# FNet and H3 in one kernel: where the items of the inverse stage stand beside the hidden-DFT pieces, and how many rounded inputs are kept ready

## The chip, the core and the metric

The kernel runs on one NeuronCore of one Trainium2 chip. The metric is the device time of one execution in microseconds (us), as the median of several runs. The core has five engines that run side by side, each with its own queue of instructions in program order: PE (TensorE, matmuls; its weight loads are shown apart as PEld), DVE (VectorE), ACT (ScalarE), POOL (GpSimd) and SP (SyncE). In this kernel SP does nothing but issue transfers, POOL issues a few transfers besides small arithmetic, and ACT issues some of the stores.

## The reference, cut to what matters

```python
x = A_x                                   # 1 x 2048 x 576, float32
x = x + A(_layernorm(x))                  # first layer
x = x + B(_layernorm(x), k, v, shift_k, ssm_k, ssm_D)
x = x + A(_layernorm(x))                  # second layer
x = x + B(_layernorm(x), k, v, shift_k, ssm_k, ssm_D)

def A(x):                                 # FNet: real part of a 2-D DFT
    a = x @ dft_hid_re.T; b = x @ dft_hid_im.T
    return dft_seq_re @ a - dft_seq_im @ b

def B(q, k, v, shift_k, ssm_k, ssm_D):    # H3
    kv = short_causal_conv(k, shift_k) * v
    y = irfft(rfft(kv, 4096) * rfft(ssm_k, 4096))[:2048] + kv * ssm_D
    return q * y
```

The factor y of B does not depend on q, so it is computed once and used in both layers.

## The kernel before, in words

The sequence is cut into 16 blocks of 128 rows. Matrix products are made in fp32r from two parts of each factor: a rounded high part, which ACT writes, and the low part that is left, which DVE gets by a subtraction. The helper `split` (L97) makes both; in the stage of interest it is `act_split` (L518), whose ACT half is issued through `act` (L511), so that all ACT instructions of the stage keep the order in which they are written.

The first layer's sequence DFT is the loop `layer` (L302): 128 steps numbered n, each with 12 matmuls 128x512 into four accumulators named s and two into one named rm. Every second step of a stretch, a **W piece** is put in (`finish`, L293; `hidden`, L278): 27 matmuls 128x288 of the hidden DFT, in a row, into one PSUM bank of the tag bk, which DVE then adds to the residual (L289). The tag bk has three banks, and the items below use them too.

Between the steps the kernel works off the long convolution as a list of 96 items, `feeds` (L570 and on), written by the generator `branch`. The middle items (64) transform, multiply and transform back; the inverse items (32, called kind 1 or inverse items here) finish the transform. Ten inverse items are spread among the last middle items, and 22 come after the last middle item, which has number 73; these are the items 74 to 95. An inverse item (`i2_products`, L552) is:

- four matmuls 128x288 into two bk banks, from a coefficient tile (`fc`, loaded by POOL, L586 through L173) and from the rounded input, high and low part (`df`);
- for each bank one ACT copy of half the partitions (L560, through L514), one DVE addition of the other half (L561) and one store by SP (L562).

After its products item i has the input of item i+2 rounded (`split_feed(i + 2)`, L618) and the raw input of item i+6 loaded by SP (`load_feed`, L577). There are three `df` tiles of 1152 words, four landing tiles, four `fc` tiles in this last part and four output tiles `vo`. The raw inputs of the items from 80 on are columns of `v_d[1]`, to which the last middle item writes too, so the load for item 80 needs the store of the last inverse product of the middle stage (L550, issued by ACT).

When an item is written into the program is set by two counters in the main loop (L788 to L818): `passed` grows by a share of 3.2 for each step and by 3.6 for each W piece, `spent` by the item's own cost (2.0 for an inverse item), and items are written as long as `spent` lags behind. At a W piece the piece is written first, 3.6 is added, and the items that have come due follow. The items' instructions are tied behind the DVE addition of the latest W piece and the latest evacuation of the accumulators (`behind(*added, *evac)`). A list scheduler then gives each engine its final order: it takes instructions in the order in which they are written, but lets one that is ready go ahead of one that its own timing model believes not yet ready.

Walking through the counters gives the order in which the last items and W pieces are written. Before the change:

| step n | written, in order, at the end of the step |
|---|---|
| 101 | item 74 inside the step; W, 75, 76 |
| 103 | item 78 inside; W, 79, 80 |
| 105 | item 83 inside; W, 84, 85 |
| 107 | item 88 inside; W, 89, 90 |
| 109 | item 92 inside; W, 93, 94 |

The other items stand inside the steps between. The last W piece of the block comes after step 110 and all items.

At the last middle item (L630) the tiles of the middle stage that are no longer needed are given to the inverse stage. One SBUF region of 6144 words holds, in this order: three `df` tiles (0 to 3456), the middle stage's matrices `mc` (3456 to 3968), two tiles `yf` of its rounded products (3968 to 4544 and 4544 to 5120), two `fc` tiles (5120 to 5632). Before the change two more `fc` tiles of 256 words are laid from 3968 on, over the first `yf`.

Of the kernel before, what the change touches and what calls it, by code (L numbers as in the profile page):

```python
# [15 lines left out]
P = 128  # L16
HP = P // 2
S = 2048
D = 576
# [26 lines left out]
I2_LATE = 6  # L46
I2_COST = 2.0
PIECE = 3.6
STEP = 3.2
KP = 4  # L50
H = 2 * P
# [15 lines left out]
def fnet_h3_kernel(ctx: ExitStack, tc: tile.TileContext, x, c_mat, w_re, w_im, k_pad, v, shift_k,  # L67
# [34 lines left out]
    @contextmanager  # L102
    def behind(*instructions):
        with ExitStack() as stack:
            for i in instructions:
                stack.enter_context(tc.issue_after(i))
            yield
# [185 lines left out]
    def finish(pending, pieces):  # L293
        while pending and pieces:
            if not isinstance(pending[0], types.GeneratorType):
                pending[0] = hidden(*pending[0])
            if next(pending[0], 0) == 0:
                pending.pop(0)
            else:
                pieces -= 1  # L300

    def layer(get_x, xres, done, pending, blocks=TB):  # L302
        steps = [(g, tb, k) for tb in range(blocks) for g in range(2) for k in range(J)]
        for n, (g, tb, k) in enumerate(steps):
            for i in range(2):
                if n == 0 and steps[i] not in CT:
                    load_c(steps[i])
            if n + 2 < len(steps):
                load_c(steps[n + 2])
            for i in range(XLEAD + 1 if blocks == TB else 1):  # L310
                if n + i < J:
                    get_x(n + i)
            if k == 0:
                ps = list(acc4)
                ps.append(psp.tile([P, NT], F32, tag="rm", name="rm"))
            c = CT.pop(steps[n])
            first, last = k == 0, k == J - 1
            while last and g == 0 and pending:
                yield n, None
            for dc in range(NC):  # L320
                xh = X[k][:, dc * P:(dc + 1) * P]
                xl = X[k][:, D + REM + dc * P:D + REM + (dc + 1) * P]
                mm(ps[dc], xh, c[0], first, False)
                mm(ps[dc], xh, c[1], False, False)
                seq[:] = [mm(ps[dc], xl, c[0], False, last)]
                if dc == NC // 2 - 1:
                    yield n, False
                elif blocks == TB and dc < NC - 1 and n >= MID_FROM and not last:
                    yield n, "part"
                if last:  # L330
                    (evac_u if blocks == TB else save_u)(g, ps, dc)
            xr = X[k][:, NC * P:D + REM]
            mm(ps[NC], xr, c[0], first, False)
            seq[:] = [mm(ps[NC], xr, c[1], False, last)]
            if last and blocks < TB:
                store_r(tb, g, ps[NC])
            elif last:
                evac_r(g, ps)
                if g == 1:
                    us = dict(U)  # L340
                    pending.extend([us, tb, jj, xres, done] for jj in range(TB))
            yield n, True
# [8 lines left out]
    def branch():  # L351
# [224 lines left out]
        def load_feed(i):  # L576
            if i < len(feeds):  # L577
                kind, hf, q = feeds[i]
                landed[i] = ring["land"]()
                load_after(two(landed[i]) if kind else landed[i], v_d[hf][:, q::J, :] if kind else  # L580
                           t_d[4 * q:4 * q + 4, :, hf * D:(hf + 1) * D].rearrange("m j d -> (m j) d"))

        def load_fc(k):
            if k < len(rows):
                fcs[k] = two(ring["fc"]())
                load_fr(fcs[k], i2c[rows[k]])  # L586

        def split_feed(i):
            if i < len(feeds):
                halves[i] = parts("df")  # L590
                act_split(*halves[i], landed.pop(i))
# [6 lines left out]
        for i in range(2):  # L598
            split_feed(i)
            load_feed(i + 3)  # L600
        used, ahead, feed_ahead, product = 0, 2, 3, None
        for i, (kind, hf, q) in enumerate(feeds):
            df = halves.pop(i)
            if kind:
                i2_products(hf, q, fcs.pop(used), df)
                load_fc(used + ahead)
                used += 1
            else:
                kk = mid_kernel(df)
                yield 1.6  # L610
                p1 = mid_signal(df, kk)
                if len(yfs) == MID_LAG:
                    yield 1.1
                    mid_inverse(*yfs.pop(0))
                if product is not None:
                    yfs.append((*product[:2], mid_round(product[2])))
                product = hf, q, p1
            split_feed(i + 2)  # L618
            if i >= I2_FIRST - 8 and feed_ahead == 3:
                tiles = [ring["land"]() for _ in range(3)]  # L620
                if tiles[0] is third:
                    ring["land"], feed_ahead = Ring(tiles[1:]), 2
                    lay(m1, fc_at, ("fc", 2 * P, 2))
                    load_fc(0)
                    load_fc(1)
            if feed_ahead == 2:
                feed_ahead = 2.5
            else:
                load_feed(i + int(feed_ahead) + 2)
            if i == last_mid:  # L630
                yfs.append((*product[:2], mid_round(product[2])))
                while yfs:
                    yield 0.4
                    mid_inverse(*yfs.pop(0))
                for name, t, at, words in (("fc", m1, spare, 2 * P), ("land", flts, kk_at, D)):
                    old = ring[name]
                    held = [old.tiles[(old.n + m) % 2] for m in range(2)]
                    fresh(name)
                    lay(t, at, (name, words, 2))
                    ring[name].tiles.extend(held)  # L640
                for m in range(2):
                    load_fc(used + ahead + m)
                    load_feed(i + ahead + 3 + m)
                ahead = feed_ahead = 4
            yield I2_COST if kind else 0.4

    def sums(src, junk):
# [140 lines left out]
    spent = passed = 0.0  # L788
    total = (I2_END + 1 - MID_FROM) * STEP + 3 * 2 * TB * PIECE
    work = 64 * 3.1 + 32 * I2_COST  # L790
    for n, whole in layer(get_x0, lambda j: x[:, j, :], done0, pending):
        part = whole == "part"
        if part:
            whole = False
        if (whole or whole is not None and n % J < J - 1) and n <= F1_END and not part:
            at = n if whole else n - 0.5
            at16 = 4 + 2 * F1_16
            want = int(4 + F1_16 * at / 8 if at <= 16 else at16 + (68 - at16) * (at - 16) / (F1_END - 16))
            with behind(made[min(n + 2, J - 1)], *evac):
                while used < want:  # L800
                    next(br)
                    used += 1
        if whole is not None and not part and n >= W_FROM and len(W) < 9:
            with behind(*stored):
                next(wl)
        if whole and n == MID_LOAD:
            with behind(*asked):
                next(br)
        if n >= MID_FROM:
            if whole is not None:  # L810
                share = (5 if whole else 3) if n % J < J - 1 else (8 if whole else 6)
                passed += STEP * share / 14 * BORDER.get(n % J, 1.085)
            if whole is None or whole and n % 2 == 1 and n % (2 * J) < J - 1 and pending:
                finish(pending, 1)
                passed += PIECE
            while spent < work * min(1.0, passed / total):
                with behind(*added, *evac):
                    spent += next(br, work)  # L818
        if not whole:
            continue  # L820
        if n >= W_SAVE and n % 2 == 0:
            next(wl, 0)
        m = n - PREP
        if m == 0:
            lay(flts, SC_AT + CRAW * NT + 2 * D, ("xa", D, 2), ("yb", D, 2))
            old = ring["craw"]
            held = [old(), old()]
            fresh("craw")
            lay(flts, SC_AT + CRAW * NT + 6 * D, ("craw", NT, 1))
            ring["craw"].tiles.extend(held)  # L830
            gate = region_b(F32, "gate")
            lay(gate, 0, ("xa", D, 4), ("yb", D, 4), ("xj", D, 2))
        if 0 <= m and n < HOLD:
            advance(m // 2 if m % 2 == 0 and m < 2 * EARLY else None)
# [340 lines left out]
```

## Time and profile before

| what | us |
|---|---|
| median of three runs (1180.59, 1182.12, 4165.63) | 1182.12 |
| the profiled execution, its own time | 1181.27 |
| its span, from the first instruction to the last | 1179.5 |
| PE busy | 1167.0 |
| DVE busy | 867.0 |
| ACT busy | 647.6 |
| POOL busy | 75.7 |

The profiled execution's own time is 1.8 us over its span. In the trace the stretch of the inverse items after item 74 goes from 538 to 597 us. Times in the views count from the start of the span. The ends of matmuls are modelled, so a matmul looks longer than the distance to the next one's start, and PE looks busy while it waits for a short time; its losses are read from the distances between starts.

### The profile page before, as it was taken

What the parts mean: (1) busy time and instruction counts of PE and PEld (TensorE: products, weight loads), DVE (VectorE), ACT (ScalarE), POOL (GpSimd) and SP (SyncE); (2) the same over time, 40 slices, a digit from 0 to 9 for tenths busy, and PEclk for the clock granted to TensorE, in tenths of its full rate; (3) what the DMA queues carried; (4) which work ended last, traced back from release to release, by engine and by line L of the source; (5) the groups of instructions that cost most, each with busy time, mean ns of one, the idle gap of its engine ahead of it and who ended that gap; (6) DMA issues with size and microseconds to landing.
All of it is one profiled execution on the core that took longest, in us unless ns stands there. A gap on an engine that the chain in (4) does not pass through costs nothing.

```text
span 1179.5 us, 18144 instructions
## 1 busy us (share of the span) xinstructions
PE 1167.0 (99%) x6198; PEld 988.8 (84%) x6198; DVE 867.0 (74%) x1564; ACT 647.6 (55%) x1280; POOL 75.7 (6%) x115
## 2 busy tenths in 40 slices
PE   8999999999999999999999999999999999999997
PEld 6776667988899888888888898888888888889997
DVE  7899983788777778877757766865776777774764
ACT  7865655577766667766645666534444445450210
POOL 2310000000000000001101111000000000001111
PEclk9999999999999999999999999999999999999999
DMA  9879898456656666648956777762762777795621
GB/s 325 297 228 308 263 292 291 156 153 177 215 196 211 198 181 193 192 140 241 286 185 215 249 250 239 241 236 89 252 240 72 233 273 259 263 323 164 201 103 41
DMA packets 147455, 255.67 MB, mean 217 GB/s; under 512 B 16161, under 2 KB 56353, under 8 KB 147362
## 3 DMA queue, kind: packets, MB, share of 16 engines
q1 hardware_dynamic: 111890, 210.17, 55.7%
q10 hardware_dynamic: 28560, 37.91, 9.1%
q0 software_dynamic: 6912, 6.43, 2.4%
q8 instruction: 49, 0.80, 0.3%
q14 instruction: 44, 0.36, 0.1%
HBM read 187.80 MB, written 66.65 MB: 216 GB/s over the span
## 4 chain that ended last, share of the span: by engine, by line
PE 90%; DVE 4%; DMA 3%; ACT 2%; issue 1%; SPq 0%; POOL 0%; DVEq 0%; ACTq 0%
PE s L76 52%; PE bk L76 29%; PE rm L76 6%; PE bf L76 2%; DMA flts<-in_ssm_k 1%; DMA t<-ud 1%; DVE f1f L395 1%; ACT flts L514 1%; DVE mid L520 0%; DVE mats L100 0%; DVE f1f L400 0%; DMA early<-in_x 0%; DVE u L100 0%; DMA vd<-flts 0%; DMA flts<-vd 0%
## 5 line engine op out<-in xcount | busy, mean ns | idle before, releaser
L76 PE MATMUL s<-mats 128*128 128x512 f32 x2102 | 549.4, 395 | 4.3 <-ACT mats L197 2.3
L76 PEld LDWEIGHTS s<-mats 128*128 128x128 f32 x2102 | 382.0, 188 | 84.6 <-issue 10.7
L100 DVE TENSOR_TENSOR mats<-flts,mats 128x512 fp32r<-128x512 f32 x206 | 140.9, 688 | 50.4 <-ACT mats L99 46.1
L99 ACT ACTIVATE mats<-flts 128x512 fp32r<-128x512 f32 x206 | 128.1, 627 | 78.9 <-PE bk L76 34.3
L514 ACT ACTIVATE flts<-bk 128x288 f32<-128x288 f32 (+1 forms) x192 | 78.5, 409 | 101.6 <-PE bk L76 83.4
L76 PE MATMUL bk<-mid 128*128 128x288 f32 x704 | 131.1, 301 | 0.3
L76 PEld LDWEIGHTS bk<-mid 128*128 128x128 f32 x704 | 110.7, 188 | 22.0 <-ACT flts L514 5.1
L76 PE MATMUL bk<-w,u 128*128 128x288 f32 x864 | 119.9, 295 | 0.1
L76 PEld LDWEIGHTS bk<-w,u 128*128 128x128 f32 x864 | 117.5, 188 | 2.7 <-ACT flts L514 0.8
L520 DVE TENSOR_TENSOR mid<-flts,mid 128x576 fp32r<-128x576 f32 (+1 forms) x149 | 92.2, 624 | 5.9 <-ACT mid L514 4.2
L76 PE MATMUL rm<-mats 128*128 128x512 f32 x304 | 94.6, 391 | 0.3 <-DVE flts L275 0.3
L514 ACT ACTIVATE mid<-flts 128x576 fp32r<-128x576 f32 (+1 forms) x148 | 79.5, 574 | 1.8 <-DVE flts L561 0.7
L289 DVE TENSOR_TENSOR flts<-flts,bk 128x288 f32<-128x288 f32 x48 | 21.8, 453 | 72.6 <-PE bk L76 72.6
L76 PE MATMUL bk<-mats 128*128 128x288 f32 (+1 forms) x376 | 67.8, 317 | 0.0
L76 PEld LDWEIGHTS rm<-mats 128*128 128x128 f32 x304 | 56.9, 188 | 12.9 <-PE s L76 0.7
L453 ACT ACTIVATE flts<-bf 128x384 f32<-128x384 f32 (+1 forms) x104 | 43.2, 462 | 43.9 <-PE bf L76 42.5
L76 PE MATMUL s<-t,mats 128*128 128x512 f32 x264 | 65.2, 390 | 0.1
L186 POOL TENSOR_TENSOR flts<-flts 128x1 f32<-128x1 f32 x34 | 28.0, 824 | 518.2 <-DVE flts L185 515.8
L76 PE MATMUL bk<-mats,t 128*128 128x288 f32 (+1 forms) x368 | 59.3, 303 | 0.0
L514 ACT ACTIVATE flts<-flts 64x288 f32<-64x288 f32 x128 | 56.7, 443 | 3.9
L76 PEld LDWEIGHTS s<-t,mats 128*128 128x128 f32 x264 | 49.4, 188 | 10.9 <-DVE t L100 0.7
L76 PEld LDWEIGHTS bk<-mats 128*128 128x128 f32 x376 | 55.5, 188 | 3.4
(152 smaller groups left out, 1495.6 us busy)
## 6 DMA issues: line engine op xcount, KB each, us to landing
flts<-in_c_mat SPq DMA_DIRECT2D x148, 256.0 KB, 3.5
ph<-in_c_mat SPq DMA_DIRECT2D x54, 512.0 KB, 4.1
flts<-in_c_mat SPq DMA_DIRECT2D x30, 512.0 KB, 5.4
flts<-td SPq DMA_DIRECT2D x53, 288.0 KB, 3.0
td<-flts ACTq DMA_DIRECT2D x36, 384.0 KB, 4.8
vd<-flts ACTq DMA_DIRECT2D x64, 144.0 KB, 3.0
flts<-vd SPq DMA_DIRECT2D x32, 288.0 KB, 4.4
ud<-ph ACTq DMA_DIRECT2D x12, 512.0 KB, 6.5
```

The source lines that it names most:

```text
L76: return nc.tensor.matmul(ps, lhsT, rhs, start=first, stop=last, skip_group_check=more).ins
L99: a = nc.scalar.activation(h, src, AF.Copy).ins
L100: return a, nc.vector.tensor_tensor(l, src, h.bitcast(F32), OP.subtract).ins
L186: pows.append(nc.gpsimd.tensor_tensor(rs, ve, mhalf, OP.pow).ins)
L289: added[:] = [nc.vector.tensor_tensor(r[:, cs], r[:, cs], ps[:, :HD], OP.add).ins]
L395: nc.vector.tensor_tensor(out_t[:, n], k, wt[3 - t][:, n], OP.mult)
L453: stored[:] = [nc.scalar.activation(so[:, i, :], ps[i], AF.Copy).ins]
L514: last_act.append(nc.scalar.activation(*args, **kw).ins)
L520: nc.vector.tensor_tensor(l, src, h.bitcast(F32), OP.subtract)
```

## The change

Three things are changed.

First, the rule at a W piece. The writing of due items becomes a function `keep_up`, which is called before the piece as well as after it. Once `spent` has reached 218.4, which is after the first item past the middle stage, half of the piece's 3.6 is credited ahead of the piece and half behind it; earlier, nothing is credited ahead, but items that are due by the step alone are now written ahead of the piece. By the counters the order becomes:

| step n | written, in order, at the end of the step |
|---|---|
| 101 | item 74 inside; 75, W, 76 |
| 103 | item 78 inside; 79, 80, W |
| 105 | item 83 inside; 84, W, 85 |
| 107 | item 88 inside; 89, W, 90 |
| 109 | item 92 inside; 93, 94, W |

Ahead of step 101 only four halves of middle items change sides at the W pieces of steps 75, 77, 97 and 99.

Second, at the last middle item a fourth `df` tile is laid over words 3456 to 4608 (`mc`, the first `yf` and 64 words of the second), the input of item 76 is rounded at once, and from then on item i has the input of item i+3 rounded.

Third, the two added `fc` tiles move from 3968 to 4608, over the second `yf`; three raw inputs instead of two are loaded at the last middle item, the third of them that of item 80, and from then on item i loads the input of item i+7.

```diff
+BEFORE = PIECE / 2
+I2_SPREAD = 10
...
-        used, ahead, feed_ahead, product = 0, 2, 3, None
+        used, ahead, feed_ahead, split_ahead, product = 0, 2, 3, 2, None
...
-            split_feed(i + 2)
+            split_feed(i + split_ahead)
...
-                for name, t, at, words in (("fc", m1, spare, 2 * P), ("land", flts, kk_at, D)):
+                old = ring["df"]
+                held = [old() for _ in range(3)]
+                fresh("df")
+                lay(m1, 6 * D, ("df", 2 * D, 1))
+                ring["df"].tiles.extend(held)
+                split_ahead = 3
+                split_feed(i + split_ahead)
+                for name, t, at, words in (("fc", m1, 8 * D, 2 * P), ("land", flts, kk_at, D)):
...
                 for m in range(2):
                     load_fc(used + ahead + m)
+                for m in range(3):
                     load_feed(i + ahead + 3 + m)
-                ahead = feed_ahead = 4
+                ahead, feed_ahead = 4, 5
...
+    def keep_up():
+        nonlocal spent
+        while spent < work * min(1.0, passed / total):
+            with behind(*added, *evac):
+                spent += next(br, work)
+
...
             if whole is None or whole and n % 2 == 1 and n % (2 * J) < J - 1 and pending:
+                ahead = BEFORE if spent >= 64 * 3.1 + I2_SPREAD * I2_COST else 0.0
+                passed += ahead
+                keep_up()
                 finish(pending, 1)
-                passed += PIECE
-            while spent < work * min(1.0, passed / total):
-                with behind(*added, *evac):
-                    spent += next(br, work)
+                passed += PIECE - ahead
+            keep_up()
```

## The prediction

> **What bounds the kernel now.** I read the page first, then the busy times of two stretches, the groups of matmuls in one of them, and last the waits and the timelines around one W piece.
>
> ```profile
> span 1179.5 us, 18144 instructions
> PE 1167.0 (99%) x6198; PEld 988.8 (84%) x6198; DVE 867.0 (74%) x1564; ACT 647.6 (55%) x1280; POOL 75.7 (6%) x115
> PEclk9999999999999999999999999999999999999999
> ```
>
> PE is the bound nearly everywhere, and its granted clock stays at the top tenth, so no edit can win anything by the clock. The change removes and adds no matmul. All it can win is PE's time lost to waiting in the stretch that it rearranges, and that has to be read from starts. The next three views give it: two stretches (the changed one, and a plain one with sequence-DFT steps alone), the matmul groups of the changed one, and the timeline of PE around two later W pieces that nothing disturbs.
>
> ```profile
> 538.07:597.39 59.32, 59.08 (x342) 51.51 (x342) 42.48 (x77) 36.02 (x73) 9.04 (x18) 1.00 0.88 251
> 601.16:655.00 53.84, 53.84 (x239) 44.55 (x239) 37.57 (x88) 31.14 (x60) 6.51 (x12) 1.00 0.64 218
> ```
> ```profile
> L76 PE MATMUL s<-mats 128*128 128x512 f32 x105 | 29.6, 393 | 0.0
> L76 PE MATMUL bk<-w,u 128*128 128x288 f32 x135 | 18.7, 295 | 0.0
> L76 PE MATMUL bk<-mid 128*128 128x288 f32 x84 | 17.9, 310 | 0.2
> L76 PE MATMUL rm<-mats 128*128 128x512 f32 x18 | 5.6, 390 | 0.0
> ```
> ```profile
> 658.14 3.71 PE L76 MATMUL bk<-w,u 128*128 128x288 f32 x27
> 661.69 2.90 PE L76 MATMUL s<-mats 128*128 128x512 f32 x12
> 664.42 0.62 PE L76 MATMUL rm<-mats 128*128 128x512 f32 x2
> 664.88 3.77 PE L76 MATMUL bk<-w,u 128*128 128x288 f32 x27
> 668.48 0.85 PE L76 MATMUL s<-mats 128*128 128x512 f32 x3
> ```
>
> The plain stretch is 17 steps of 14 matmuls (the 239th is cut by the edge): 53.84 / 238 = 0.226 us for a 128x512. The two W pieces take 661.69 - 658.14 = 3.55 and 668.48 - 664.88 = 3.60, in the mean 3.575 / 27 = 0.1324 us for a 128x288. The changed stretch, from the start of one W piece to that of the fifth after it, holds 105 + 18 = 123 of the first and 135 + 84 = 219 of the second: 123 x 0.226 + 219 x 0.1324 = 27.8 + 29.0 = 56.8 us. It lasts 59.32. So PE loses **2.5 us** here, and this is nearly all that there is to win, 0.2% of the time. What the losses wait for is told by the weight loads, which wait ahead of their matmuls:
>
> ```profile
> PEld bk L76 <- DVE mid L520: 0.8, 2, 0.4
> PEld bk L76 <- DVE flts L561: 0.7, 4, 0.2
> PEld bk L76 <- ACT mid L514: 0.6, 2, 0.3
> PEld bk L76 <- ACT flts L514: 0.2, 1, 0.2
> ```
>
> L520 and the ACT line into mid are the rounding of an item's input: 0.8 + 0.6 = 1.4 us. L561 and the ACT line into flts empty PSUM banks: 0.7 + 0.2 = 0.9 us. Together 2.3 of the 2.5. Where the rounding comes late is seen at any W piece; here the one that ends at 553.46, on PE and ACT:
>
> ```profile
> 553.46 0.68 PE L76 MATMUL bk<-mid 128*128 128x288 f32 x4
> 553.99 0.40 PE L76 MATMUL s<-mats 128*128 128x512 f32 x1
> 554.22 0.50 PE L76 MATMUL bk<-mid 128*128 128x288 f32 x2
> 554.56 0.62 PE L76 MATMUL s<-mats 128*128 128x512 f32 x2
> 555.02 0.90 PE L76 MATMUL bk<-mid 128*128 128x288 f32 x3
> ```
> ```profile
> 547.39 0.83 ACT L514 ACTIVATE flts<-bk 64x288 f32<-64x288 f32 x2
> 548.56 0.69 ACT L514 ACTIVATE mid<-flts 128x576 fp32r<-128x576 f32 x1 [0.33 <-DMA flts<-vd]
> 553.92 0.84 ACT L514 ACTIVATE flts<-bk 64x288 f32<-64x288 f32 x2 [3.45 <-DMA flts<-vd]
> 554.78 0.68 ACT L514 ACTIVATE mid<-flts 128x576 fp32r<-128x576 f32 x1
> ```
> ACT idles 3.45 us while PE runs the W piece, because everything that it has to do next stands behind item 79, whose matmuls come after it. Then three items follow within 2 us of PE time; the rounding for item 81 starts at 554.78 only, and PE waits for it inside the group at 555.02 (three matmuls in 0.90 us).
>
> **The change part by part.** *Items ahead of a W piece.* Seven of the 22 items move (75, 79, 80, 84, 89, 93, 94), with all that they issue: four matmuls, two ACT copies, one ACT rounding, two DVE additions, one DVE subtraction, two stores and a load on SP, one load on POOL. The prices of these for the whole stretch:
>
> ```profile
> L514 ACT ACTIVATE flts<-bk 64x288 f32<-64x288 f32 x44 | 17.9, 406 | 19.0 <-PE bk L76 14.7 <-DMA flts<-vd 3.5
> L514 ACT ACTIVATE mid<-flts 128x576 fp32r<-128x576 f32 x20 | 13.7, 686 | 1.4 <-DVE flts L561 0.7 <-DMA flts<-vd 0.3
> L561 DVE TENSOR_TENSOR flts<-bk,flts 64x288 f32<-64x288 f32 x44 | 20.0, 456 | 3.2 <-ACT flts L514 1.9
> L520 DVE TENSOR_TENSOR mid<-flts,mid 128x576 fp32r<-128x576 f32 x20 | 15.2, 759 | 2.0 <-ACT mid L514 1.6
> L289 DVE TENSOR_TENSOR flts<-flts,bk 128x288 f32<-128x288 f32 x5 | 2.3, 454 | 10.8 <-PE bk L76 10.8
> ```
>
> One item costs ACT 2 x 0.406 + 0.686 = 1.50 us and DVE 2 x 0.456 + 0.759 = 1.67 us. DVE idles 10.8 / 5 = 2.2 us under each W piece, so one item's work fits there (and two items' work, 3.34 us, not quite, at steps 103 and 109). After the piece only one item follows at once. The items' additions are tied behind the addition of the W piece written before, which is long done; L289 itself now stands behind up to 3.3 us of DVE work that begins with the piece, and its own matmuls take 3.6 us, so it is not late. SP issues the moved items' stores earlier, POOL the coefficient loads.
>
> *Rounding three ahead.* Same instructions, one item earlier. The 1.4 us of waits for rounded inputs are bounded by 0 (ACT is busy again without a pause right after each piece, in the rows at 553.92 and 554.78) and by 1.4 (the rounding is done at least one item, 1.5 us of ACT, earlier, and the longest of these waits is 0.4). I take all **-1.4**. The 0.9 us for PSUM banks I leave as they are: two items still follow each other closely, now ahead of the piece, and three banks are still three.
>
> *The first extra rounding* stands behind the last inverse product, for which ACT waits anyhow, and ahead of item 74's two copies: these come 0.69 us later, and with them the banks for item 75 and the W piece. PE has the steps' own matmuls to put there (they are independent), so 0, up to 0.7 if they were in the wrong order.
>
> *The load for item 80* cannot come earlier: it needs the last store of the middle stage. On SP:
>
> ```profile
> 537.69 0.33 SPq L169 DMA_DIRECT2D flts<-in_c_mat  x1
> 538.79 1.12 SPq L562 DMA_DIRECT2D yb<-flts  x2
> 545.04 0.56 SPq L169 DMA_DIRECT2D flts<-vd  x1
> ```
> ```profile
> SPq L169 <- DMA vd<-flts: 5.0, 2, 4.6
> ```
>
> SP waits 4.6 us for that store and issues the load at 545.04; ACT's rounding at 548.56 waits for it already now. It stands behind item 78's copies (547.39). After the change it stands ahead of them, so they wait until 548.56 + 0.69 = 549.25 in place of 547.39: 1.86 us of lateness on ACT and in the banks of item 78, with items 79 and 80 and a W piece next in line. Between item 78 and the W piece PE has step matmuls:
>
> ```profile
> 547.34 2.23 PE L76 MATMUL s<-mats 128*128 128x512 f32 x9
> ```
>
> That is 9 x 0.226 = 2.0 us of cover ahead of item 79, so the price lies between 0 and 1.9; nearest is the row that shows the cover, and I take **+0.5** for items 79 and 80 in a row behind it. What is queued behind SP's wait (stores of item 75, the load for item 81) is so already.
>
> *The moved coefficient tiles.* POOL issues the loads for items 76 and 77 once the inverse products that read the old tiles are done:
>
> ```profile
> 536.27 1.06 POOL L173 DMA_DIRECT2D mid<-in_i2c  x2 [43.67 <-PE rm L76]
> 537.57 0.53 POOL L173 DMA_DIRECT2D mid<-in_i2c  x1 [0.24 <-PE bk L76]
> ```
> ```profile
> DMA to landing us min/median/max: 2.3/4.1/7.6
> ```
>
> Before, the new tiles lay over the first yf, read by the last product but one; now over the second, read by the last. Both loads must wait until about 537.6, and one may go behind the third (537.57 + 0.53 = 538.1). With the landing times of this stretch (2.3, 4.1, 7.6) item 76's tile is there at 540.4, 542.2 or 545.7. PE wants it after item 75 and the W piece that now starts at 538.07 + 4 x 0.1324 = 538.6 or later, so not before 542.2. The price is 0 up to 3.5; I take the median, **0**, since the later banks push the W piece back too.
>
> [...]
>
> *The rest.* Four halves of middle items change sides earlier, where the middle stage keeps its order otherwise: 0, within 0.3 either way. Behind 601 us nothing is written differently.
>
> **The sum** is made against the profiled execution, 1181.27 us (span 1179.5; the median of the runs, 1182.12, lies 0.85 above it, the fastest 0.7 below): 1181.27 - 1.4 + 0.5 = **1180.4 us**.
>
> **The rivals.** *The waits move only.* If the three PSUM banks are the limit, two items in a row ahead of the piece wait for banks as they did behind it, and PE waits for a bank where it waited for a rounded input: 1181.3. For it: 0.9 of the waits are banks already. Against: each long wait (0.3, 0.4) names the rounding. [...]
>
> *All waits go.* With ACT and DVE filled under every W piece the banks come free in time too, and nothing is lost at item 80: 1181.27 - 2.5 = 1178.8.
>
> *The coefficients come late.* This ends on the other side. PE stands in order at item 76 until the tile lands; at 7.6 us (545.7) that is 3.5 us, so 1181.27 - 1.4 + 3.5 = 1183.4; from a landing of 543.6 on, which is a stall of 1.4, it eats the gain. For it: the DMA share is 0.88 through the stretch. Against: the median.
>
> **How the numbers follow.** The likeliest, most rounding waits gone with a small loss at item 80, has a chance of 0.5 and by itself 1179.5 to 1181.0. Waits move only: 0.2. All go: 0.1. Coefficients late (or more than 1.4 lost at item 80): 0.2. The range takes in the ends, 1178.8 to 1183.4. No case reaches 2%, or 23.6 us, which is about what a measurement of this kernel can tell from no change: the whole loss of the stretch is 2.5, and the largest price 3.5. I leave 0.01 for faster and 0.02 for slower, for an order of the scheduler that differs far beyond these places.
>
> **What would show it.** In the stretch after 538 the waits for L520 and for ACT into mid should be gone from the weight loads' rows, those for L561 should stay near 0.7, DVE's idle time before L289 should fall from 10.8 us to under 4, and ACT should wait around 546 to 548.5 for the load of item 80. The prediction is wrong if PE stands still after the W piece at about 542 (then the coefficients), if the rounding waits stay, or if the stretch between the same two W pieces is longer than 59.32.

## The result, and the profile after

The changed kernel takes 1179.3 us (median; 1177.69 to 1181.44) where the kernel before takes 1180.73 in the same comparison, 22 runs of each (one of the runs before took 4165.63 us and has no part in the ratio): a ratio of 0.9987, with an interval of 0.9982 to 0.9993. That is 1.4 us less, within 2%, beside a forecast of 1180.4 us and a sum of -0.9. The prediction held 2% for about what a measurement of this kernel can tell from no change; this interval is 0.11% wide. The profiled execution took 1179.43 us, with a span of 1176.7, against 1181.27 and 1179.5.

To set two kernels side by side in the changed stretch one needs two ends between which PE does the same work. The two W pieces of the prediction don't serve, since items have moved across them. From the first matmul of step 97 to that of step 111 every kernel below has the same matmuls, and this stretch is the measure from here on. Before, it runs from 504.34 to 601.00, **96.65 us** (by the starts before they are rounded); in the changed kernel it takes **95.22**. The first fence is the timeline of PE of the kernel before at the two ends, the second the busy times of the changed kernel from end to end (length, then the busy times of PE, its weight loads, DVE, ACT and POOL, the granted clock, the DMA share, GB/s).

```profile
504.34 1.54 PE L76 MATMUL s<-mats 128*128 128x512 f32 x6
...
601.00 1.31 PE L76 MATMUL s<-mats 128*128 128x512 f32 x5
```
```profile
503.42:598.64 95.22, 94.84 (x565) 84.85 (x564) 69.30 (x129) 58.80 (x122) 10.56 (x20) 1.00 0.74 217
```

96.65 - 95.22 = 1.43 us, as much as the medians differ. (The spans of the two executions differ by 2.8 us. Of this 0.9 lies ahead of the stretch, where two profiles of the changed kernel differ by 0.7 among themselves: it begins at 503.42 in one and at 504.08 in the other.) The starts of the matmuls show where PE stood in this stretch. Before, there were four gaps of 0.21 to 0.24 us, with about 0.1 more in the matmul behind each: 1.3 us, all for rounded inputs, at the items that follow a W piece. Now there are three, all for PSUM banks. The same answer from the weight loads of the changed kernel, and DVE's groups:

```profile
PEld bk L78 <- DVE flts L563: 1.7, 3, 0.6
PEld bk L78 <- ACT flts L516: 0.2, 1, 0.2
```
```profile
L563 DVE TENSOR_TENSOR flts<-bk,flts 64x288 f32<-64x288 f32 x44 | 20.0, 455 | 3.6 <-ACT flts L516 2.4
L291 DVE TENSOR_TENSOR flts<-flts,bk 128x288 f32<-128x288 f32 x5 | 2.3, 454 | 7.7 <-PE bk L78 7.7
```

The rows for the rounding, 0.8 and 0.6 us before, are gone. L563 (L561 before; all lines here are two further on), which empties banks, has risen from 0.7 us to 1.7. The timeline of PE shows the three places: two rows that name L563, and one, at 588.31, that starts later than its forerunner allows (four matmuls of 0.226 us are 0.90, and it starts 1.10 us after the first of them).

```profile
539.09 3.73 PE L78 MATMUL bk<-w,u 128*128 128x288 f32 x27
542.66 0.68 PE L78 MATMUL bk<-mid 128*128 128x288 f32 x4
...
545.18 0.63 PE L78 MATMUL s<-mats 128*128 128x512 f32 x2
546.00 0.53 PE L78 MATMUL bk<-mid 128*128 128x288 f32 x2 [0.19 <-DVE flts L563]
...
548.41 0.97 PE L78 MATMUL bk<-mid 128*128 128x288 f32 x6
549.22 1.33 PE L78 MATMUL s<-mats 128*128 128x512 f32 x5
550.73 0.54 PE L78 MATMUL bk<-mid 128*128 128x288 f32 x2 [0.19 <-DVE flts L563]
551.11 0.39 PE L78 MATMUL s<-mats 128*128 128x512 f32 x1
551.34 3.77 PE L78 MATMUL bk<-w,u 128*128 128x288 f32 x27
...
587.21 1.09 PE L78 MATMUL s<-mats 128*128 128x512 f32 x4
588.31 0.54 PE L78 MATMUL bk<-mid 128*128 128x288 f32 x2
```

The gap at 546.00 lies after the items that follow the first W piece, those at 550.73 and 588.31 at the second of two items ahead of one piece (steps 103 and 109). By the starts they cost 0.36, 0.36 and 0.17 us, and about 0.1 more each in the matmul behind them: 1.2 us, nearly as much as the four gaps of before.

So what the change won lies beside the gaps. Take the stretch in two parts, ahead of and behind the seventh s matmul of step 100, up to which all kernels have the same matmuls again. First the kernel before, then the changed one:

```profile
529.64 1.54 PE L76 MATMUL s<-mats 128*128 128x512 f32 x6
```
```profile
528.34 1.53 PE L78 MATMUL s<-mats 128*128 128x512 f32 x6
```

Behind it the time falls from 71.36 to 70.30 us. Besides the gaps, fifteen matmuls there start 0.05 to 0.11 us late in the kernel before, 1.3 us in all; in the changed kernel there are four of them, 0.3 us. About half of those of before stand behind a weight load that waits for a bank. Ahead of it the time falls from 25.29 to 24.92 us, though no inverse item has moved there, only halves of middle items at the W pieces of steps 97 and 99. The other such halves, at the pieces of steps 75 and 77, lie ahead of the stretch: from step 74 to step 81 it was 44.69 us and is 44.41. Every kernel below with the new main loop has 24.92 to 24.96 and 44.36 to 44.44 us at these two places, and the two with the old one 25.26 and 25.27, and 44.69 and 44.72. So 0.6 us go with these halves, half of it inside the stretch, though no run moves them by themselves. Which of the three edits did the rest is what the experiments ask.

### The profile page after: what moved, and what is told of

Its sections match the earlier page's. It is cut to its first block, busy times and chain, and to the rows that moved or that the text cites. A ratio compares the mean times of both kernels' runs of the same rounds, so it can differ in the third digit from the quotient of the medians.

```text
span 1176.7 us, 18141 instructions
## 1 busy us (share of the span) xinstructions
PE 1165.3 (99%) x6198; PEld 989.5 (84%) x6198; DVE 868.1 (74%) x1564; ACT 647.4 (55%) x1280; POOL 75.5 (6%) x115
## 4 chain that ended last, share of the span: by engine, by line
PE 93%; DVE 3%; DMA 2%; ACT 1%; issue 1%; SPq 0%; POOL 0%; DVEq 0%; ACTq 0%
PE s L78 54%; PE bk L78 30%; PE rm L78 6%; PE bf L78 2%; DVE f1f L397 1%; DVE f1f L402 0%; DVE mats L102 0%; DVE u L102 0%; ACT flts L516 0%; DMA early<-in_x 0%; DMA flts<-vd 0%; DMA flts<-in_ssm_k 0%; DMA vd<-flts 0%; DMA td<-flts 0%; DVE f1r L102 0%
## 5 line engine op out<-in xcount | busy, mean ns | idle before, releaser
L78 PE MATMUL bk<-mid 128*128 128x288 f32 x704 | 128.1, 299 | 0.5 <-DVE flts L563 0.4
L291 DVE TENSOR_TENSOR flts<-flts,bk 128x288 f32<-128x288 f32 x48 | 21.7, 453 | 64.3 <-PE bk L78 64.3
L78 PEld LDWEIGHTS s<-t,mats 128*128 128x128 f32 x264 | 49.4, 188 | 10.8 <-DVE t L102 0.6
```

Source lines behind the costliest of these rows:

```text
L78: return nc.tensor.matmul(ps, lhsT, rhs, start=first, stop=last, skip_group_check=more).ins
L291: added[:] = [nc.vector.tensor_tensor(r[:, cs], r[:, cs], ps[:, :HD], OP.add).ins]
```

## The experiments

Three theories stood against each other. *Buffer*: the fourth tile and the earlier rounding took the waits away, as the prediction's sum has it. *Order*: items on both sides of the piece took them away, and the buffer does nothing. *Banks*: any gain ends at the three PSUM banks, wherever two items follow each other closely. Every table gives the time of the kernel, its ratio to the kernel before, and the stretch of steps 97 to 111 in its profile.

### The change in two halves

The first kernel has the new order only (`keep_up`, `BEFORE`, `I2_SPREAD` in the main loop) with three tiles and rounding two ahead. The second has the tile, the rounding three ahead, the moved coefficient tiles and the third load, with the main loop of before:

```diff
 # order only, against the kernel before
+                ahead = BEFORE if spent >= 64 * 3.1 + I2_SPREAD * I2_COST else 0.0
+                passed += ahead
+                keep_up()
                 finish(pending, 1)
-                passed += PIECE
+                passed += PIECE - ahead
...
```
```diff
 # buffer only, against the changed kernel
-                ahead = BEFORE if spent >= 64 * 3.1 + I2_SPREAD * I2_COST else 0.0
-                passed += ahead
-                keep_up()
                 finish(pending, 1)
-                passed += PIECE - ahead
+                passed += PIECE
...
```

> The items stand on both sides of the W pieces as in the change, but there are three input buffers, inputs are rounded two items ahead, and loads and coefficient tiles are as before. Measure: from the first matmul of step 97 to that of step 111, which hold the same matmuls in every version (before 504.34 to 601.00 = 96.66 us, changed 503.42 to 598.64 = 95.22 us). If the order makes the gain (ACT and DVE get work under the W piece), the stretch is 95.2 to 95.6 us and few waits for rounded inputs are left on the weight loads. If the fourth buffer makes it, the stretch is 96.2 to 96.7 us and these waits stay above 1.0 us.

> The fourth buffer, rounding three items ahead, the third early load and the moved coefficient tiles as in the change, but the main loop of before: each W piece is written ahead of the items that are due. If the order makes the gain, the stretch from step 97 to step 111 is 96.2 to 96.7 us, and ACT and DVE idle under each W piece as before (10 us of DVE before L291 over five pieces). If the buffer makes it, the stretch is 95.2 to 95.6 us with no wait for rounded inputs, only waits for banks.

| kernel | us | ratio | stretch |
|---|---|---|---|
| order only | 1180.15 | 0.9992 (0.9983 to 1.0001) | 95.19 |
| buffer only | 1182.64 | 1.0016 (1.0007 to 1.0025) | 99.47 |

The order alone has the stretch of the whole change, though in the whole time it is not told apart from the kernel before. The buffer alone makes the stretch 2.8 us longer, which neither of its two ranges had. PE in the order-only kernel waits once for rounding, for item 80, whose input comes late (its load waits for the last store of the middle stage, 3.6 us of SP's time). In the buffer-only kernel PE stands still for 2.03 us. Weight loads of order only, then PE of buffer only:

```profile
PEld bk L78 <- DVE flts L563: 0.9, 3, 0.4
PEld bk L78 <- DVE mid L522: 0.6, 1, 0.6
```
```profile
541.94 0.69 PE L78 MATMUL bk<-mid 128*128 128x288 f32 x4
542.47 0.40 PE L78 MATMUL s<-mats 128*128 128x512 f32 x1
544.73 0.50 PE L78 MATMUL bk<-mid 128*128 128x288 f32 x2 [1.86 <-DVE mid L522]
```

The row names the rounding. But the second of POOL's loads, that of item 76's coefficients, was issued at 538.3 in this kernel and took 6.3 us: 544.6, just ahead of the restart at 544.73. The next experiment tells which of the two it was.

### The coefficient tiles put where they can be loaded early

At words 5632 and on nothing is laid that the last inverse product still reads, so the loads need not wait for it. The same edit is made in the buffer-only kernel, and in two others below:

```diff
-for name, t, at, words in (("fc", m1, 8 * D, 2 * P), ("land", flts, kk_at, D)):
+for name, t, at, words in (("fc", m1, fc_at + 4 * P, 2 * P), ("land", flts, kk_at, D)):
```

> e2 with the two added coefficient tiles laid over words that nobody else uses (5632 to 6144), so that their loads wait for no inverse product. In e2 PE stands still for 2.03 us at item 76, right after the W piece, and runs at a lower granted clock for some us after it; the view names the rounding (L522), the landing of the second coefficient load at 544.59 lies 0.14 us ahead of the restart. If the coefficients are the cause, standstill and slow clock go and the stretch falls from 99.47 to 95.8 to 96.6 us. If the rounding is, it stays above 98.5 us.

It took 1180.46 us, 0.9999 (0.999 to 1.0007), and the standstill is gone: shown to be the coefficients, not the rounding that the row named. Its stretch and its weight loads:

```profile
504.53:600.84 96.31, 95.95 (x565) 84.76 (x564) 68.44 (x129) 58.53 (x122) 9.50 (x18) 1.00 0.74 212
```
```profile
PEld bk L78 <- DVE flts L563: 1.9, 5, 0.6
PEld bk L78 <- ACT flts L516: 0.5, 2, 0.2
```

Here is the buffer by itself: no wait for rounding is left, the waits for banks are 1.9 us in place of 0.7, and the stretch is 96.31 in place of 96.65. All but 0.3 us of the waits has only moved.

### How many items ahead of the piece

A limit of one item ahead of a piece, in the changed kernel and in the order-only one, and the other extreme, the whole piece credited ahead of it:

```diff
 # one ahead
-    def keep_up():
+    def keep_up(items=work):
...
-        while spent < work * min(1.0, passed / total):
+        while items > 0 and spent < work * min(1.0, passed / total):
+            items -= 1
...
-                keep_up()
+                keep_up(1 if ahead else work)
```
```diff
 # all ahead, in the changed kernel
-BEFORE = PIECE / 2
+BEFORE = PIECE
```

> The change, but at most one item is written ahead of a W piece once the half credit is in force, so that steps 103 and 109 have one item on each side in place of two ahead. In the changed kernel PE loses about 0.47, 0.47 and 0.28 us at three places, all with two items in a row, all for a bank that DVE's addition empties. If two items in a row are the cause, the stretch from step 97 to 111 falls from 95.2 to 94.2 to 94.6 us and these waits go. If three banks are too few at any order, it stays at 95.0 to 95.4 us.

> One item on each side of every W piece (as in e3), but without the fourth buffer: three input buffers, inputs rounded two items ahead, coefficient tiles where they were. If the order alone makes the gain, the stretch from step 97 to step 111 is 94.4 to 95.0 us (e3: 94.55). If the fourth buffer is needed once the order is right, waits for rounded inputs of 0.6 us or more are left and the stretch is 95.2 to 95.8 us.

> The change, but all of the piece's 3.6 is credited ahead of it, so that every W piece has its two items in a row ahead and none behind. If two items in a row cost a wait for a bank each time (0.3 to 0.5 us) wherever they stand, the stretch from step 97 to 111 is 96.0 to 96.6 us, the gain mostly lost. If only work under the W piece counts, it is 95.0 to 95.5 us.

| kernel | us | ratio | stretch |
|---|---|---|---|
| changed, one ahead | 1178.64 | 0.998 (0.9971 to 0.9989) | 94.55 |
| order only, one ahead | 1178.49 | 0.998 (0.9971 to 0.9989) | 94.10 |
| changed, all ahead | 1184.71 | 1.0028 (1.0016 to 1.0041) | 101.50 |

One item ahead takes the gaps at steps 103 and 109 away; without the buffer no gap over 0.15 us is left, and the stretch is 2.55 us shorter than before, 2.2 of it behind the seventh s matmul of step 100. That is 0.3 below the range that was expected for it. These are the busy times of order only, one ahead (PE is busy for all of the 94.11 us that the view gives), and its DVE group:

```profile
503.14:597.25 94.11, 94.11 (x566) 85.15 (x565) 69.25 (x129) 58.87 (x122) 10.56 (x20) 1.00 0.76 220
```
```profile
L291 DVE TENSOR_TENSOR flts<-flts,bk 128x288 f32<-128x288 f32 x5 | 2.3, 455 | 5.1 <-PE bk L78 5.1
```

With all items ahead the stretch is far outside both ranges: PE stands still for 3.19 us, here for the coefficients by name, and is slow after it. PE, then its clock (seventh term, 0.90, 0.50, 0.68, 1.00):

```profile
539.27 0.40 PE L78 MATMUL s<-mats 128*128 128x512 f32 x1
542.68 0.82 PE L78 MATMUL bk<-mid 128*128 128x288 f32 x2 [3.02 <-DMA mid<-in_i2c]
...
545.49 5.19 PE L78 MATMUL bk<-w,u 128*128 128x288 f32 x27
```
```profile
539.20:542.60 3.40, 0.46 (x3) 0.12 (x1) 2.49 (x5) 1.79 (x4) 0.53 (x1) 0.90 1.10 319
542.60:545.50 2.90, 2.82 (x9) 2.46 (x10) 0.46 (x1) 1.24 (x3) 0.00 (x0) 0.50 0.58 156
545.50:550.50 5.00, 5.00 (x28) 5.00 (x27) 1.81 (x3) 0.89 (x2) 0.53 (x1) 0.68 0.88 235
550.50:556.00 5.50, 5.50 (x32) 4.61 (x30) 4.68 (x9) 4.55 (x10) 1.58 (x3) 1.00 0.53 149
```

### What the buffer costs

The one-ahead kernels differ by the buffer and what comes with it, 94.55 against 94.10. Two kernels ask what part of it costs: the changed one with one ahead and the freed coefficient tiles, and the same kernel (tiles as changed) whose extra rounding and third load stand behind item 74's products in place of ahead of its copies. With them goes the all-ahead kernel with freed tiles.

```diff
 # late extra, against changed with one ahead
+            if i == last_mid + 1:
+                split_feed(i + 2)
+                load_feed(i + 6)
             split_feed(i + split_ahead)
...
                 split_ahead = 3
-                split_feed(i + split_ahead)
...
-                for m in range(3):
+                for m in range(2):
```

> e3 (one item on each side, fourth buffer) with the coefficient tiles over the free words. In e3 item 76 comes about 1.0 us after its coefficients have landed, so nothing should be won: stretch 94.3 to 94.8 us. If the late loads cost something that the trace does not show, it falls below 94.2 us.

> e3 (one item on each side, fourth buffer, three ahead) with one thing moved: the extra rounding, of item 76's input, and the third load, of item 80's, stand behind item 74's products in place of ahead of them. PE's order becomes that of e5, with the W piece of step 101 behind four step matmuls in place of eight. If the extra rounding ahead of item 74's copies is what delays the banks, pushes that W piece back and bunches items 76 to 78 behind it, the wait of 0.34 us at 545.94 goes and the stretch falls from 94.55 to 94.0 to 94.3 us, as e5 without the fourth buffer (94.10). If the fourth buffer costs something by itself, it stays at 94.5 or more.

> e4 (both items ahead of each W piece) with the coefficient tiles over the free words. If the 3.19 us standstill of e4 at item 76 and the slow clock after it come from the coefficients, they go, and what is left is the price of two items in a row ahead of each piece: the stretch falls from 101.50 to 95.4 to 96.2 us, with waits for banks of 0.2 to 0.4 us at each of the five pieces. If it stays above 100 us, the cause is the order itself.

| kernel | us | ratio | stretch |
|---|---|---|---|
| one ahead, freed tiles | 1178.68 | 0.9983 (0.9975 to 0.9992) | 94.53 |
| one ahead, late extra | 1179.6 | 0.9988 (0.998 to 0.9997) | 95.28 |
| all ahead, freed tiles | 1181.08 | 1.0002 (0.9993 to 1.0011) | 96.58 |

The freed tiles change nothing with one item ahead, so in that kernel the coefficients land in time: the 0.45 us are not theirs. (The margin of 1.0 us written above was too generous; item 76's load lands some 0.3 us ahead of its use.) With the extra rounding moved late, the order of PE's matmuls becomes that of the order-only kernel with one ahead, and the bank wait after the first piece is gone. That ties the bank wait to the place of the extra rounding or of the third load, which moved with it. Its time can't be read from this kernel, since PE then reaches item 76 earlier than its coefficients (issued 538.0, 6.1 us to landing) and stands for 1.11 us:

```profile
539.59 3.71 PE L78 MATMUL bk<-w,u 128*128 128x288 f32 x27
544.25 0.77 PE L78 MATMUL bk<-mid 128*128 128x288 f32 x4 [0.95 <-DMA mid<-in_i2c]
```

All ahead with the tiles freed loses 0.97 us at the first piece and 0.17 to 0.26 at each of four others to banks, one wait at each piece, and its stretch of 96.58 is that of the kernel before: the rival of the banks by itself. The first of these waits is over twice what was expected, which puts the stretch over its range of 95.4 to 96.2.

```profile
PEld bk L78 <- DVE flts L563: 3.3, 6, 1.2
```

### The late load of item 80

In the order-only kernel, items 80 to 95 read the columns of the first half in place of their own, whose last store lies further back. This changes what these items compute and leaves their number as it is.

```diff
-                load_after(two(landed[i]) if kind else landed[i], v_d[hf][:, q::J, :] if kind else
+                load_after(two(landed[i]) if kind else landed[i], v_d[0][:, q::J, :] if kind else
...
```

> e1 (order as changed, three buffers) whose inverse items 80 to 95 read the first half's columns, so that the load for item 80 needs no store of the last middle item; the part of the computation left wrong by this is the second half of the columns of y. In e1 SP waits 3.6 us for that store, ACT waits 0.91 us at 548.11 for the load of item 80, and PE loses 0.66 us at 548.85. If the store is the cause, all three go and the stretch falls from 95.19 to 94.3 to 94.7 us. If two items in a row ahead of the piece are, PE still loses 0.4 us or more there and the stretch stays at 94.9 or more.

It took 1179.85 us, 0.9988 (0.9978 to 0.9997), with a stretch of 94.78 in place of 95.19. These are ACT's rounding of item 80 in the order-only kernel and in this one; then PE's wait for it here:

```profile
548.11 0.69 ACT L516 ACTIVATE mid<-flts 128x576 fp32r<-128x576 f32 x1 [0.91 <-DMA flts<-vd]
```
```profile
547.39 0.69 ACT L516 ACTIVATE mid<-flts 128x576 fp32r<-128x576 f32 x1
```
```profile
PEld bk L78 <- DVE mid L522: 0.3, 1, 0.3
```

ACT's wait of 0.91 us is gone, and 0.41 of PE's time with it; a gap of 0.27 stays, still for the rounding of item 80. The stretch lies between the two ranges, so neither reading has it all. That the rest belongs to two items in a row is borne out by the order-only kernel with one item ahead: there the load for item 80 is issued just as late (40.5 us after the first matmul of step 97 in both kernels), item 80 stands behind the W piece, and the gap is gone altogether.

### The best version and the change once more

> The version of e5 once more, beside the changed kernel on the same chip: its time should lie 0.5 to 1.2 us under that of the changed kernel, and its stretch at 94.0 to 94.3 us, if the trace of e5 was no single case; if it was, the stretch is above 94.8 us.

> The changed kernel itself once more, to see how far the stretch from step 97 to step 111 differs from one execution to the next: 95.0 to 95.5 us, with waits for banks behind items in a row at steps 103, 104 and 110, if these are of its order; if they were of the one execution, they stand elsewhere.

Beside the same runs of the kernel before (1181.04 us) order only with one ahead took 1178.87, 0.9978 (0.997 to 0.9987), with a stretch of 94.17, and the changed kernel 1179.81, 0.9989 (0.998 to 0.9997), with 95.38. The repeat of the changed kernel has its three gaps at the same items as the first (0.37, 0.48 and 0.17 us). Stretches repeat within 0.2 us in these two pairs, so the differences of 0.4 and more above are taken as differences. In the whole time the intervals of the two overlap; what separates them is the stretch, 1.1 to 1.2 us in both pairs. The new order with at most one item ahead of a piece, and no fourth buffer, is the version with the shortest stretch and the lowest median, though in the whole time it is not told apart from the changed kernel with one ahead.

## Why the prediction was right, and where its steps were not

- **The loss of 2.5 us** has one matmul too many in it: the view counts 342 in the window, and one 128x512 of them began ahead of it. With 122 of these it is 59.32 - 122 x 0.226 - 219 x 0.1324 = 2.7 us. The version without a gap is 2.2 us shorter in the part of the stretch that matches this, so nearly all of it could be won.
- **"Rounding three ahead", -1.4.** The waits for rounded inputs went, 1.4 us to 0. But the step named the wrong edit: the order takes all of them but item 80's 0.6, and the buffer by itself turns them into waits for banks (0.7 to 1.9), which leaves 0.3 us of gain. The figure was right for these waits (1.3 us by PE's starts), and the cause that they went without others in their place was the order.
- **"The 0.9 us for PSUM banks I leave as they are."** These waits did not stay: most of the small late starts of before went (1.3 to 0.3 us by PE's starts, the unnamed ones with them), and three long waits for banks came, 1.2 us (L563 from 0.7 to 1.7 us on the weight loads): at two items in a row ahead of one piece (steps 103 and 109, which go with the limit of one) and after the first piece. The prediction saw that two items do "not quite" fit under a piece and put no price on it.
- **"The first extra rounding", 0 up to 0.7.** About 0.45 us, the difference of the one-ahead kernels with and without the buffer and its edits. The extra rounding stands ahead of item 74's copies, the scheduler puts the W piece of step 101 behind eleven of the steps' own matmuls (after the inverse products) in place of seven, and items 76 to 78 then follow closely, with the gap at 546.00. That it is the rounding and not the third load, which was moved with it, is argued from this order and not shown.
- **"The load for item 80", +0.5.** Not paid in the changed kernel. The step that failed is "cannot come earlier": ACT issued the last store of the middle stage at 536.54, right behind the extra rounding, in place of 538.01, and it took 5.5 us to land in place of 6.9. So SP waited 2.4 us for it in place of 4.6 and issued the load at 542.12, which is 38.7 us after the start of step 97 in place of 40.7. ACT has no wait for it at 546 to 548.5, and PE waits for no rounding. The price is real in the order-only kernel: 0.66 us at item 80, of which 0.4 are the load's.

```profile
SPq L171 <- DMA vd<-flts: 2.4, 1, 2.4
```

- **"The moved coefficient tiles", 0.** Right, by 0.46 us. The second of three loads is issued at 536.62 and lands 5.6 us later, at 542.2; PE wants it at 542.66. (In the repeat of the changed kernel the margin is 0.26 us.) This is POOL's row in the changed kernel and the time of that load:

```profile
536.10 1.59 POOL L175 DMA_DIRECT2D mid<-in_i2c  x3 [44.42 <-PE bk L78]
```
```profile
DMA to landing us min/median/max: 5.6/5.6/5.6
```

  What covered it is what the prediction gave as its reason: the late banks push the W piece back. Where this cover is less, the rival came true: 2.03, 3.19 and 1.11 us of standstill in the buffer-only, all-ahead and late-extra kernels. A chance of 0.2 was not too high.
- **DVE's idle time before L291** fell from 10.8 us to 7.7, not under 4; to 5.1 with one ahead and no buffer.
- **"Four halves of middle items", 0, within 0.3.** 0.6 us go with them: 0.37 at steps 97 and 99 (25.29 to 24.92) and 0.28 at steps 75 and 77 (44.69 to 44.41), in every kernel with the new main loop. The term was put at nothing because the middle stage keeps its order otherwise; the W pieces of this stage lose time to banks too, 0.4 us on the weight loads of steps 97 to 100 before and none after.

So the sum of -0.9 came near the measured -1.4 (0.8 to 2.1 by the interval of the ratio), but not by its own terms. In the part that the sum is about, behind step 100, the traces give -1.1: the gaps for rounding went, -1.3, gaps for banks came, +1.2, and small late starts went, -1.0. The +0.5 at item 80 was not paid, and the middle items gave -0.6 that the sum lacks. It is luck that these errors cancel in part and the total came near.

## What to carry to other kernels

Where PE waits for operands behind a long group of its own matmuls, look first at what the other engines have to do while the group runs: one item of evacuation work written ahead of each group took away every gap over 0.15 us, two in a row ran into the three banks, and a further input buffer only turned one wait into another. Before moving a tile to make room, find who still reads the old place last and when its first load can then be issued; here the space for the buffer cost the coefficients their lead, and the kernel kept 0.46 us of it by luck of its order. When a change bundles several edits, run each alone, with the side effect of its place in memory taken out, before saying which of them paid, and measure the parts that were put at nothing as well: here they held 0.6 us.

## What the runs showed of the hardware

**Two standstills of PE, of 2.03 and 3.19 us, cost more than themselves.** After 3.19 us without matmuls a W piece took 5.19 us in place of 3.7. The granted clock was 0.50 in the mean for 2.9 us and 0.68 for 5.0 more (rows above). These means mix two values: the clock was 1.00 up to 541.89, 0.50 from 542.68 to 548.72, and 1.00 again from there on. By the 0.90 of the first row above it fell at 542.60 - 3.40 x 0.10 / 0.50 = 541.9, an estimate, while PE still stood.

```profile
539.27:541.89 2.62, 0.39 (x3) 0.05 (x1) 2.26 (x4) 1.73 (x4) 0.53 (x1) 1.00 1.21 355
542.68:548.72 6.04, 6.04 (x22) 5.65 (x23) 2.27 (x4) 2.13 (x4) 0.53 (x1) 0.50 0.76 205
548.72:552.00 3.28, 3.28 (x24) 3.02 (x23) 1.00 (x3) 0.97 (x3) 0.49 (x1) 1.00 0.45 121
```

Against the kernel with freed tiles (0.97 us at that place) the stretch is 4.92 us longer, of which 3.19 - 0.97 = 2.22 are the standstill and 2.7 are left for the slow matmuls; with matmuls of twice the length at 0.50, an estimate, the rows above give 6.04 x 0.50 = 3.0. In the buffer-only kernel a standstill of 2.03 us was followed by it too. There the clock fell 1.0 us after PE had started again, and stayed at 0.50 for 3.4 us, half as long as in the other kernel (541.9 to 548.72); two matmuls 128x512 took 548.01 - 547.16 = 0.85 us in it, in place of 2 x 0.226 = 0.45:

```profile
544.73:545.73 1.00, 1.00 (x6) 0.91 (x7) 0.03 (x2) 0.41 (x1) 0.00 (x0) 1.00 0.11 25
545.73:549.15 3.42, 3.42 (x12) 2.96 (x11) 2.10 (x4) 1.90 (x4) 0.69 (x2) 0.50 1.01 262
549.15:552.00 2.85, 2.85 (x15) 2.43 (x15) 2.51 (x5) 2.51 (x5) 0.90 (x2) 1.00 0.94 235
```
```profile
547.16 1.06 PE L78 MATMUL s<-mats 128*128 128x512 f32 x2
548.01 0.69 PE L78 MATMUL bk<-mid 128*128 128x288 f32 x2
```

Its stretch is 99.47 - 96.31 = 3.16 us longer than with freed tiles, 1.69 of it standstill (2.03 - 0.34) and 1.5 the slow matmuls. A gap of 1.11 us (late extra) was followed by no slow matmuls: the eight 128x512 and two 128x288 from 545.36 on took 2.13 us, where the prediction's rates give 8 x 0.226 + 2 x 0.1324 = 2.07. So the prediction's price for late coefficients, the bare standstill of 3.5 us, left out a loss that was 2.7 us in the nearest case measured, 3.19. What sets the slow clock off is not shown by these runs.

**Who is named as the releaser** can be the wrong one of two. The rows of the buffer-only kernel named the rounding for the 2.03 us (1.86 of it; the weight loads' view named the banks for 2.2), and it was the load, as the kernel with freed tiles showed (0.34 us at that place).

**The coefficient loads of 128 KB that were read out above took 5.6 to 6.3 us to land**, each the second of three in a row on POOL: between the 4.1 that the prediction took as the median and the maximum of 7.6.
